# A retention layer and a bilinear feed-forward layer on one core: 36 uniform chunks instead of 40, stages placed back from their deadline, a rearranged opening, and q and k transposed by crossbar DMA from chunk 9 on

## The chip, the cores and the metric

The kernel runs on one core of one Trainium2 chip. The metric is device time in microseconds (us). A "run" is one execution; each kernel was executed several times on the same chip as the kernel before. The "span" of a profile is the time from the first to the last instruction in it; the time of the profiled run is about 2 us longer.

## The reference

There are 8 batches of 576 positions, with 8 heads of 64. First comes a retention layer (attention without softmax, with a decay per head), then a feed-forward layer in which two projections are multiplied:

```python
scores = (1 / sqrt(64)) * q @ k.transpose(0, 1, 3, 2)
gamma  = 1 - 2.0 ** (-5 - arange(8))                  # one per head
rel    = pos[:, None] - pos[None, :]
Dmat   = where(rel >= 0, gamma ** rel, 0)             # causal decay
x      = (scores * Dmat) @ v                          # -> [4608 tokens, 512]
out    = ((x @ w_a) * (x @ w_b)) @ w_out              # d_ff = 1536
```

Everything arrives and leaves as float32. The kernel computes in bfloat16.

## The kernel before

The kernel handles retention in chunks of positions. The decay is split into a factor per row of v (`vs`), a factor per column of the output (`qs`), and a 0/1 causal mask, so a chunk needs: a cast of q, k and v to bf16; q and k transposed (eight 128x128 transposes on PE into one PSUM tile, then a copy to SBUF); the running state `kv` (k times v, summed over earlier chunks of the batch); the scores; the mask multiply on DVE; the outputs (from scores, and from the state); and the multiply by `qs` that writes `xT`. 576 is 4.5 times 128, so each batch has four full chunks and a half one: 40 chunks.

The feed-forward layer takes tokens in blocks. `pa` and `pb` are the two projections, `po` the last one. It is called the dense part below. One unit is one matmul with 512 columns; a block of 512 tokens has 144 units, all of them 1296. The stages of later chunks are interleaved into the dense part: a list `todo` says after how many units which stage is put into PE's stream. In the first block the places are fixed by hand, in the later ones they are spread evenly.

```python
NCH = (S + 127) // 128
chunks = [(b, c, c * 128, min(128, S - c * 128))
          for b in range(B) for c in range(NCH)]

def transposes(i, act):
    ...                                   # cut: names
    tp = ps_att.tile([128, 2, HP, 128], BF16, tag="att", name="tp")
    for p in range(HP):
        for w, src in ((0, qb), (1, kb)):
            nc.tensor.transpose(tp[:, w, p, 0:n],
                                src[0:n, p * 128:(p + 1) * 128],
                                identity[0:n, 0:n])
    qkT = qkt_pool.tile([128, 2, HP, 128], BF16, tag="qkT", name="qkT")
    if act:
        nc.scalar.copy(qkT[:, :, :, 0:n], tp[:, :, :, 0:n])
    else:
        nc.vector.tensor_copy(qkT[:, :, :, 0:n], tp[:, :, :, 0:n])

# the opening: chunks 0 to 3, before the dense part
cast(0, early=True)                       # early: q on ACT, k on DVE
transposes(0, act=True)
for p in range(1, HP):
    make_qs(p)
state(0)
scores(0)
for i in range(1, 4):
    cast(i, early=True)
    ...                                   # cut: weight load
    transposes(i, act=True)
    flush()                               # the masks and xT multiplies put off
    outputs(i - 1)
    state(i)
    scores(i)
    flush()
...                                       # cut: weight loads
outputs(3)
flush()

# stages of the later chunks (after the first block), spread evenly over the block before theirs
gap = total / max(1, len(mine))
for m in range(len(mine)):
    p0 = m * gap
    todo += [(p0 + 0.03 * gap, "T", m), (p0 + 0.25 * gap, "S", m),
             (p0 + 0.85 * gap, "A", m)]   # transposes, scores, outputs
```

## Time and profile before

| | before |
|---|---|
| time, median (lowest to highest of 4 runs) | 390.06 us (388.33 to 390.63) |
| span of the profile | 386.2 us |
| first dense matmul | 26.9 us |
| PE transposes | 320 matmuls, 23.8 us busy |
| a 512-token block of the dense part, with the stages in it | 36.8 to 38.5 us with two groups of two chunks, 35.6 us in the last with only three chunks, 44.3 and 44.4 us where three groups of chunks fall in it |

These are lines of the page of the kernel before. In the first, the columns are busy time, share of the span and number of instructions for each engine. The next cut the span into 40 equal slices: busy share of PE in tenths, and the clock that the throttle granted to TensorE, in tenths. The last is the chain of work that ended last, by engine.

```profile
PE 351.9 (91%) x2736; PEld 188.3 (49%) x2736; DVE 169.9 (44%) x294; ACT 126.0 (33%) x242; POOL 91.4 (24%) x131
...
PE   2669996998979889899999998999998989999995
...
PEclk9999999899999999999999999999999999999999
...
PE 89%; DVE 7%; issue 1%; ACT 1%; DMA 1%; SPq 0%; DVEq 0%
```

PE is the bottleneck: what takes time away from PE, or waits away from before it, is worth its whole size. The waits of PE follow, from the view that lists who waited for whom: engine and line that waited, what it waited for, us in total, number of times, longest.

```profile
PE pa L275 <- DVE xT L262: 10.4, 8, 2.0
PE tp L188 <- ACT qb L170: 9.2, 4, 4.8
PE o L248 <- DVE sT L231: 6.3, 8, 2.0
```

The first line is the start of a block: its first `pa` matmul needs the last `xT`. The chain in order of time (start, us, what) shows one such start:

```profile
229.51 1.85 PE po L297 x8
...
231.38 0.69 DVE osb L308
232.07 0.61 DVE xT L262
...
232.72 1.02 PE pa L275 x4
```

The `xT` multiply was put off and stands behind the copy `osb` in DVE's queue. PE needs both to be done and stands still for 1.38 us.

### The profile page before, as it was taken

The numbers are of one execution on the slowest core, as the hardware profiler recorded it, in microseconds if no ns is written. First come the engines' busy times: TensorE is split into PE (matmuls) and PEld (weight loads), VectorE is DVE, ScalarE is ACT, GpSimd is POOL, SyncE is SP. The second block draws the span as 40 slices with busy tenths as digits, with TensorE's granted clock in tenths as the row PEclk, the third lists the DMA queues.
The fourth block names the chain that finished last, engine by engine and source line by source line (L and its number), as shares of the span: only waits on it lengthen the run. The fifth ranks groups of instructions, "written<-read, shape, count | busy, mean of one in ns | idle before, by whom it ended". The sixth has DMA issues, their size and how long they took to land.

```text
span 386.2 us, 6892 instructions
## 1 busy us (share of the span) xinstructions
PE 351.9 (91%) x2736; PEld 188.3 (49%) x2736; DVE 169.9 (44%) x294; ACT 126.0 (33%) x242; POOL 91.4 (24%) x131
## 2 busy tenths in 40 slices
PE   2669996998979889899999998999998989999995
PEld 1444454866744544445454544454544544444442
DVE  4443434344734454455335623662455444523321
ACT  6523322523414422234142414231433214312320
POOL 2640355413430430404132221122140300000000
PEclk9999999899999999999999999999999999999999
DMA  9999999957939902890268029602820020011002
GB/s 179 188 206 207 182 223 192 259 99 161 195 93 205 168 1 81 161 196 0 83 147 168 2 81 186 129 3 81 187 47 0 30 81 2 0 49 61 3 20 89
DMA packets 122512, 42.91 MB, mean 111 GB/s; under 512 B 113264, under 2 KB 117872, under 8 KB 122480
## 3 DMA queue, kind: packets, MB, share of 16 engines
q1 hardware_dynamic: 117728, 37.76, 46.5%
q0 software_dynamic: 4752, 4.72, 7.6%
q8 instruction: 21, 0.34, 0.4%
q14 instruction: 11, 0.09, 0.1%
HBM read 37.75 MB, written 9.44 MB: 122 GB/s over the span
## 4 chain that ended last, share of the span: by engine, by line
PE 89%; DVE 7%; issue 1%; ACT 1%; DMA 1%; SPq 0%; DVEq 0%
PE pa L275 25%; PE po L297 25%; PE pb L285 24%; PE tp L188 5%; PE o L248 3%; DVE xT L262 2%; PE kv L208 2%; PE o L256 2%; DVE sT L231 2%; DVE osb L308 1%; DMA kf<-in_k_dram 1%; DVE hT L290 1%; ACT qs L133 1%; DVE kb L171 0%; ACT qb L170 0%
## 5 line engine op out<-in xcount | busy, mean ns | idle before, releaser
L290 DVE TENSOR_TENSOR hT<-ha,pb 128x512 bf16<-128x512 bf16 (+1 forms) x120 | 76.1, 634 | 117.0 <-PE pb L285 115.0
L275 PE MATMUL pa<-xT,wa_sb 128*128 128x512 bf16 (+1 forms) x480 | 114.3, 361 | 10.5 <-DVE xT L262 10.4
L281 ACT CAST ha<-pa 128x512 bf16<-128x512 f32 (+1 forms) x120 | 65.0, 542 | 159.2 <-PE pa L275 159.0
L285 PE MATMUL pb<-xT,wb_sb 128*128 128x512 bf16 (+1 forms) x480 | 114.0, 360 | 0.2 <-ACT ha L281 0.2
L297 PE MATMUL po<-wo_sb,hT 128*128 128x512 bf16 x432 | 97.5, 380 | 0.0
L175 POOL TENSOR_TENSOR vb<-vf,vs 128x512 bf16<-128x512 f32 (+1 forms) x40 | 41.6, 1040 | 162.6 <-PE o L248 110.2
L275 PEld LDWEIGHTS <-wa_sb 128*128 128x128 bf16 x480 | 45.0, 98 | 53.9 <-issue 13.2
L285 PEld LDWEIGHTS <-wb_sb 128*128 128x128 bf16 x480 | 47.3, 98 | 47.8 <-issue 1.4
L297 PEld LDWEIGHTS <-hT 128*128 128x128 bf16 x432 | 40.5, 98 | 47.3
L308 DVE COPY osb<-po 128x512 f32<-128x512 f32 x18 | 12.5, 692 | 54.1 <-PE po L297 54.1
L262 DVE TENSOR_TENSOR xT<-o,qs 128x512 bf16<-128x512 f32 (+1 forms) x40 | 24.7, 631 | 23.1 <-PE o L256 18.0
L173 POOL CAST qb<-qf 128x512 bf16<-128x512 f32 (+1 forms) x36 | 21.9, 607 | 41.6 <-DMA qf<-in_q_dram 20.9
L188 PE MATMUL tp<-identity,qb 128*128 128x128 bf16 (+1 forms) x160 | 22.1, 228 | 9.2 <-ACT qb L170 9.2
L193 ACT COPY qkT<-tp 128x1024 bf16<-128x1024 bf16 (+1 forms) x23 | 21.2, 920 | 26.2 <-PE tp L188 26.2
L306 ACT COPY osb<-po 128x512 f32<-128x512 f32 x18 | 10.5, 585 | 57.4 <-PE po L297 57.4
L188 PE MATMUL tp<-identity,kb 128*128 128x128 bf16 (+1 forms) x160 | 21.8, 227 | 1.8 <-DVE kb L171 1.8
L174 POOL CAST kb<-kf 128x512 bf16<-128x512 f32 (+1 forms) x36 | 22.0, 611 | 6.3 <-DMA kf<-in_k_dram 3.7
L248 PE MATMUL o<-sT,vb 128*64 128x128 bf16 (+1 forms) x320 | 17.1, 226 | 6.3 <-DVE sT L231 6.3
L188 PEld LDWEIGHTS <-qb 128*128 128x128 bf16 (+1 forms) x160 | 15.4, 103 | 13.9 <-ACT qb L170 10.0
L248 PEld LDWEIGHTS <-vb 128*64 128x64 bf16 (+1 forms) x320 | 11.1, 114 | 15.2 <-issue 14.8
L188 PEld LDWEIGHTS <-kb 128*128 128x128 bf16 (+1 forms) x160 | 15.7, 104 | 3.9 <-DVE kb L171 2.4
L195 DVE COPY qkT<-tp 128x1024 bf16<-128x1024 bf16 (+1 forms) x17 | 10.9, 641 | 10.0 <-PE tp L188 9.4
(206 smaller groups left out, 181.7 us busy)
## 6 DMA issues: line engine op xcount, KB each, us to landing
out_dram<-osb SPq DMA_DIRECT2D x36, 256.0 KB, 2.0
qf<-in_q_dram SPq DMA_DIRECT2D x32, 256.0 KB, 4.9
kf<-in_k_dram SPq DMA_DIRECT2D x32, 256.0 KB, 5.0
vf<-in_v_dram SPq DMA_DIRECT2D x32, 256.0 KB, 5.1
wo_sb<-in_moe_w_out_dram POOLq DMA_DIRECT2D x3, 512.0 KB, 17.3
qf<-in_q_dram SPq DMA_DIRECT2D x8, 128.0 KB, 4.9
kf<-in_k_dram SPq DMA_DIRECT2D x8, 128.0 KB, 4.5
vf<-in_v_dram SPq DMA_DIRECT2D x8, 128.0 KB, 4.4
```

The lines of the kernel that those rows point to most:

```text
L173: nc.gpsimd.tensor_copy(qb[0:n, :], qf[0:n, :])
L174: nc.gpsimd.tensor_copy(kb[0:n, :], kf[0:n, :])
L175: nc.gpsimd.tensor_tensor(vb[0:n, :].rearrange("p (h d) -> p h d", h=H), vf[0:n, :].rearrange("p (h d) -> p h d", h=H), vs[0:n, c, :].unsq ...
L188: nc.tensor.transpose(tp[:, w, p, 0:n], src[0:n, p * 128:(p + 1) * 128], identity[0:n, 0:n])
L193: nc.scalar.copy(qkT[:, :, :, 0:n], tp[:, :, :, 0:n])
L248: nc.tensor.matmul(o[64 * hi:64 * hi + 64, p, 0:n], vb[0:n, e0:e0 + 64], sT[0:n, hi, p, 0:n], start=(p == 0), stop=(c == 0), skip_group_ch ...
L262: later.append(lambda: nc.vector.tensor_tensor(xT[:, :, t0:t0 + n], o[:, :, 0:n], qs[:, :, s0:s0 + n], op=ALU.mult))
L275: nc.tensor.matmul(pa[:, 0:n], wa_sb[:, c, fs], xT[:, c, tok0:tok0 + n], start=(c == 0), stop=(c == NC - 1))
L281: nc.scalar.copy(ha[:, 0:n], pa[:, 0:n])
L285: nc.tensor.matmul(pb[:, 0:n], wb_sb[:, c, fs], xT[:, c, tok0:tok0 + n], start=(c == 0), stop=(c == NC - 1))
L290: nc.vector.tensor_tensor(hT[:, F, 0:n], ha[:, 0:n], pb[:, 0:n], op=ALU.mult)
L297: nc.tensor.matmul(po, hT[:, F, u * 128:(u + 1) * 128], wo_sb[:, F, :], start=(F == 0), stop=(F == NF - 1))
```

## The change

It does four things. (1) Chunks of 128 run over two batches at a time, so 1152 positions make nine chunks, the middle one half from each batch, with a mask of its own. (2) The opening is one loop, and the copies out of PSUM are split, q on ACT and k on DVE. (3) Each stage from chunk 9 on is placed counting back from its block: outputs 16 units before the block starts, scores 36 units before that, casts 104 before. Chunks 4 to 8 get fixed positions. (4) From chunk 9 on, one DMA per chunk transposes q and k through the crossbar, from SBUF to SBUF.

```diff
-    NCH = (S + 127) // 128
+    NCH = NTOK // 128
+    PER = 2 * S // 128
+    MID = PER // 2
...                                        (cut: rows of a chunk, two-part loads)
+    def turn(i):
+        qkT = qkt_pool.tile([128, 2, HP, 128], BF16, tag="qkT", name="qkT")
+        nc.sync.dma_start_transpose(
+            qkT.rearrange("p w c s -> p (w c) s"),
+            natural[i][0].rearrange("p w d -> p (w d)"))
+        transposed[i] = qkT
...                                        (in transposes)
-        if act:
-            nc.scalar.copy(qkT[:, :, :, 0:n], tp[:, :, :, 0:n])
+        if how == "both":
+            nc.scalar.copy(qkT[:, 0], tp[:, 0])
+            nc.vector.tensor_copy(qkT[:, 1], tp[:, 1])
...                                        (opening; casts of chunk 0 before it)
+    for i in range(4):
+        transposes(i, "both")
+        scores(i)
+        state(i)
+        flush()
+        if i < 3:
+            cast(i + 1, early=True)
+        outputs(i)
+        flush()
...                                        (stages of the later chunks)
+    FIRST_TURNED = 9
+    def ahead(upto, early=False):
+        while counts["cast"] <= min(upto, NCH - 1):
+            i = counts["cast"]
+            cast(i, early)
+            counts["cast"] += 1
+            if counts["load"] < NCH:
+                load(counts["load"])
+                counts["load"] += 1
+            if i >= FIRST_TURNED:
+                turn(i)
...
+    for i in range(NCH - 1, 8, -2):
+        g = (i, i + 1) if i + 1 < NCH else (i,)
+        third = min(starts[i] - 16, limit - 60)
+        limit = third
+        second = third - (26 if i == 9 else 36)
+        todo += [(max(176, third - 104), ahead, (g[-1],)),
+                 (second - 16, first_stage, (g,)),
+                 (second, second_stage, (g,)),
+                 (third, third_stage, (g,))]
+    for i, first, second, third in (
+            (4, 117, 122, 129), (5, 134, 138, 143), (6, 147, 151, 158),
+            (7, 160, 164, 172), (8, 175, 179, 188)):
+        todo += [(first, one_by_one, ("T", i)), (second, one_by_one, ("S", i)),
+                 (third, one_by_one, ("A", i))]
```

In the first block, the `pa` matmuls of 3, 4 and 5 column groups run before the matching `pb`. Blocks are 512, 256, 384, 384, then 512, where before had 512, 256, 256, then 512.

More of the change, by code (lines that the diff above doesn't have):

```diff
@@ L47, with rows_of @@
     gammas = [1.0 - 2.0 ** (-5.0 - h) for h in range(H)]
-    NCH = (S + 127) // 128
-    chunks = [(b, c, c * 128, min(128, S - c * 128))
-              for b in range(B) for c in range(NCH)]
-    NTB = NTOK // 512
+    NCH = NTOK // 128
+    PER = 2 * S // 128
+    MID = PER // 2
+    HALF = S - 128 * MID
+    assert HALF == 64 and NTOK % (2 * S) == 0
+    def rows_of(i):
+        b, m = 2 * (i // PER), i % PER
+        if m < MID:
+            return [(0, 128, b, 128 * m)]
+        if m == MID:
+            return [(0, 64, b, 128 * m), (64, 64, b + 1, 0)]
+        return [(0, 128, b + 1, 64 + 128 * (m - MID - 1))]
     def pool(name, bufs, space=None):
@@ L61 @@
     nat = pool("nat", 5)
-    qkt_pool = pool("qkt", 4)
+    qkt_pool = pool("qkt", 6)
     st_pool = pool("st", 4)
     h_pool = pool("hT", 2)
-    ha_pool = pool("ha", 3)
+    ha_pool = pool("ha", 6)
     o_pool = pool("osb", 4)
@@ L85, in load @@
     def load(i):
-        if i >= len(chunks):
+        if i >= NCH:
             return
-        b, c, s0, n = chunks[i]
         tiles = []
@@ L91, in load @@
             t = stage.tile([128, DM], FP32, tag=name, name=name)
-            nc.sync.dma_start(
-                t[0:n, :].rearrange("p (h d) -> p h d", h=H),
-                src[b, :, s0:s0 + n, :].rearrange("h s d -> s h d"))
+            for r0, n, b, s0 in rows_of(i):
+                nc.sync.dma_start(
+                    t[r0:r0 + n, :].rearrange("p (h d) -> p h d", h=H),
+                    src[b, :, s0:s0 + n, :].rearrange("h s d -> s h d"))
             tiles.append(t)
@@ L99 @@
         load(i)
+    idxp_i = const.tile([128, PER], INT32)
+    nc.gpsimd.iota(idxp_i[:, 0:MID + 1], pattern=[[128, MID + 1]], base=0,
+                   channel_multiplier=1)
+    nc.gpsimd.iota(idxp_i[:, MID + 1:PER], pattern=[[128, PER - MID - 1]],
+                   base=64, channel_multiplier=1)
+    idx_i = const.tile([128, S + 64], INT32)
+    nc.gpsimd.iota(idx_i[:, 0:S], pattern=[[1, S]], base=0,
+                   channel_multiplier=0)
+    nc.gpsimd.iota(idx_i[:, S:S + 64], pattern=[[1, 64]], base=0,
+                   channel_multiplier=0)
     identity = const.tile([128, 128], BF16)
     make_identity(nc, identity)
-    idxp_i = const.tile([128, NCH], INT32)
-    nc.gpsimd.iota(idxp_i, pattern=[[128, NCH]], base=0, channel_multiplier=1)
-    idx_i = const.tile([128, S], INT32)
-    nc.gpsimd.iota(idx_i, pattern=[[1, S]], base=0, channel_multiplier=0)
     mask = const.tile([128, 128], BF16)
@@ L113 @@
         base=0, pattern=[[1, 128]], channel_multiplier=-1)
-    idxp_f = const.tile([128, NCH], FP32)
-    nc.vector.tensor_copy(idxp_f, idxp_i)
-    vs = const.tile([128, NCH, H], FP32)
-    for h in range(H):
-        nc.scalar.activation(vs[:, :, h], idxp_f, AF.Exp,
-                             bias=0.0, scale=-math.log(gammas[h]))
+    mask2 = const.tile([128, 128], BF16)
+    nc.gpsimd.tensor_copy(mask2, mask)
+    nc.gpsimd.memset(mask2[0:64, 64:128], 0.0)
     lgp = const.tile([128, HP], FP32)
@@ L127 @@
     nc.vector.memset(biasq, math.log(scale))
-    idx_f = const.tile([128, S], FP32)
+    idxp_f = const.tile([128, PER], FP32)
+    nc.vector.tensor_copy(idxp_f, idxp_i)
+    nc.vector.tensor_scalar_add(idxp_f[64:128, MID:MID + 1],
+                                idxp_f[64:128, MID:MID + 1], -float(S))
+    vs = const.tile([128, PER, H], FP32)
+    for h in range(H):
+        nc.scalar.activation(vs[:, :, h], idxp_f, AF.Exp,
+                             bias=0.0, scale=-math.log(gammas[h]))
+    idx_f = const.tile([128, S + 64], FP32)
     nc.vector.tensor_copy(idx_f, idx_i)
-    qs = const.tile([128, HP, S], FP32)
+    qs = const.tile([128, HP, S + 64], FP32)
     def make_qs(c):
@@ L134, in make_qs @@
                              bias=biasq[:, 0:1], scale=lgp[:, c:c + 1])
-    make_qs(0)
     states = [const.tile([128, HP, 128], BF16, name=f"state{i}")
@@ L162, in cast @@
     def cast(i, early=False):
-        if i >= len(chunks):
-            return
-        b, c, s0, n = chunks[i]
         qf, kf, vf = staged.pop(i)
-        qb, kb, vb = (nat.tile([128, DM], BF16, tag=t, name=t)
-                      for t in ("qb", "kb", "vb"))
+        qkb = nat.tile([128, 2, DM], BF16, tag="qkb", name="qkb")
+        vb = nat.tile([128, DM], BF16, tag="vb", name="vb")
+        qb, kb = qkb[:, 0], qkb[:, 1]
         if early:
-            nc.scalar.copy(qb[0:n, :], qf[0:n, :])
-            nc.vector.tensor_copy(kb[0:n, :], kf[0:n, :])
-        else:
-            nc.gpsimd.tensor_copy(qb[0:n, :], qf[0:n, :])
-            nc.gpsimd.tensor_copy(kb[0:n, :], kf[0:n, :])
+            nc.scalar.copy(qb, qf)
+            nc.vector.tensor_copy(kb, kf)
+        else:
+            nc.gpsimd.tensor_copy(qb, qf)
+            nc.gpsimd.tensor_copy(kb, kf)
@@ L175, in cast @@
         nc.gpsimd.tensor_tensor(
-            vb[0:n, :].rearrange("p (h d) -> p h d", h=H),
-            vf[0:n, :].rearrange("p (h d) -> p h d", h=H),
-            vs[0:n, c, :].unsqueeze(2).to_broadcast([n, H, D]),
+            vb.rearrange("p (h d) -> p h d", h=H),
+            vf.rearrange("p (h d) -> p h d", h=H),
+            vs[:, i % PER, :].unsqueeze(2).to_broadcast([128, H, D]),
             op=ALU.mult)
-        natural[i] = (qb, kb, vb)
-    def transposes(i, act):
-        b, c, s0, n = chunks[i]
-        qb, kb, vb = natural[i]
-        tp = ps_att.tile([128, 2, HP, 128], BF16, tag="att", name="tp")
-        for p in range(HP):
-            for w, src in ((0, qb), (1, kb)):
-                nc.tensor.transpose(tp[:, w, p, 0:n],
-                                    src[0:n, p * 128:(p + 1) * 128],
-                                    identity[0:n, 0:n])
-        qkT = qkt_pool.tile([128, 2, HP, 128], BF16, tag="qkT", name="qkT")
-        if act:
-            nc.scalar.copy(qkT[:, :, :, 0:n], tp[:, :, :, 0:n])
+        natural[i] = (qkb, qb, kb, vb)
@@ new lines, in turn, with transposes @@
+    def turn(i):
[4 more added lines that the diff above has]
+        transposed[i] = qkT
+    def transposes(i, how):
+        qkb, qb, kb, vb = natural[i]
+        tp = ps_att.tile([128, 2, HP, 128], BF16, tag="att", name="tp")
+        for w, src in ((0, qb), (1, kb)):
+            for p in range(HP):
+                nc.tensor.transpose(tp[:, w, p, :],
+                                    src[:, p * 128:(p + 1) * 128], identity)
+        qkT = qkt_pool.tile([128, 2, HP, 128], BF16, tag="qkT", name="qkT")
+        if how == "both":
+            nc.scalar.copy(qkT[:, 0], tp[:, 0])
+            nc.vector.tensor_copy(qkT[:, 1], tp[:, 1])
+        elif how == "act":
+            nc.scalar.copy(qkT, tp)
@@ L194, in transposes @@
         else:
-            nc.vector.tensor_copy(qkT[:, :, :, 0:n], tp[:, :, :, 0:n])
+            nc.vector.tensor_copy(qkT, tp)
         transposed[i] = qkT
     def state(i):
-        b, c, s0, n = chunks[i]
-        if c == NCH - 1:
+        m = i % PER
+        if m == PER - 1:
             return
-        qb, kb, vb = natural[i]
-        if c == 0:
-            kv_of[b] = ps_kv.tile([128, HP, 128], FP32, tag="kv", name="kv")
-        kv = kv_of[b]
+        qkb, qb, kb, vb = natural[i]
+        r = slice(64, 128) if m == MID else slice(0, 128)
@@ L206, in state @@
+        if m == 0 or m == MID:
+            kv_of[0] = ps_kv.tile([128, HP, 128], FP32, tag="kv", name="kv")
+        kv = kv_of[0]
         for p in range(HP):
             sl = slice(p * 128, (p + 1) * 128)
-            nc.tensor.matmul(kv[:, p, :], kb[0:n, sl], vb[0:n, sl],
-                             start=(c == 0 and p == 0), stop=True,
+            nc.tensor.matmul(kv[:, p, :], kb[r, sl], vb[r, sl],
+                             start=(m in (0, MID) and p == 0), stop=True,
                              skip_group_check=True)
@@ L216, in scores @@
     def scores(i):
-        b, c, s0, n = chunks[i]
         qkT = transposed[i]
@@ L225, in scores @@
                 r = slice(64 * hi, 64 * hi + 64)
-                nc.tensor.matmul(ps[hi][0:n, p, 0:n], qkT[r, 1, p, 0:n],
-                                 qkT[r, 0, p, 0:n], start=True, stop=True,
+                nc.tensor.matmul(ps[hi][:, p, :], qkT[r, 1, p, :],
+                                 qkT[r, 0, p, :], start=True, stop=True,
                                  skip_group_check=True)
+        keep = mask2 if i % PER == MID else mask
         def masked(hi):
             nc.vector.tensor_tensor(
-                sT[0:n, hi, :, 0:n], ps[hi][0:n, :, 0:n],
-                mask[0:n, 0:n].unsqueeze(1).to_broadcast([n, HP, n]),
+                sT[:, hi], ps[hi],
+                keep.unsqueeze(1).to_broadcast([128, HP, 128]),
                 op=ALU.mult)
@@ L239, in outputs @@
     def outputs(i):
-        b, c, s0, n = chunks[i]
-        qb, kb, vb = natural.pop(i)
+        m = i % PER
+        qkb, qb, kb, vb = natural.pop(i)
         qkT = transposed.pop(i)
@@ L247, in outputs @@
                 e0 = p * 128 + 64 * hi
-                nc.tensor.matmul(o[64 * hi:64 * hi + 64, p, 0:n],
-                                 vb[0:n, e0:e0 + 64], sT[0:n, hi, p, 0:n],
-                                 start=(p == 0), stop=(c == 0),
+                nc.tensor.matmul(o[64 * hi:64 * hi + 64, p, :],
+                                 vb[:, e0:e0 + 64], sT[:, hi, p, :],
+                                 start=(p == 0), stop=(m == 0),
                                  skip_group_check=True)
-        if c > 0:
+        if m > 0:
             st = state_of.pop(i)
+            n = 64 if m == MID else 128
             for p in range(HP):
@@ L260, in outputs @@
                                      skip_group_check=True)
-        t0 = b * S + s0
+        s0 = rows_of(i)[0][3]
         later.append(lambda: nc.vector.tensor_tensor(
-            xT[:, :, t0:t0 + n], o[:, :, 0:n], qs[:, :, s0:s0 + n],
+            xT[:, :, i * 128:(i + 1) * 128], o, qs[:, :, s0:s0 + 128],
             op=ALU.mult))
-    blocks = [512, 256, 256] + [512] * ((NTOK - 1024) // 512)
-    def ffn_block(tok0, n):
+    blocks = [512, 256, 384, 384] + [512] * ((NTOK - 1536) // 512)
@@ L270, in ffn_block @@
+    WCOLS = [3, 4, 5]
+    def ffn_block(tok0, n, runs):
         hT = h_pool.tile([128, NF, 512], BF16, tag="h", name="hT")
-        for F in range(NF):
-            fs = slice(F * 128, (F + 1) * 128)
-            pa = ps_ffn.tile([128, 512], FP32, tag="ab", name="pa")
-            for c in range(NC):
-                nc.tensor.matmul(pa[:, 0:n], wa_sb[:, c, fs],
-                                 xT[:, c, tok0:tok0 + n],
-                                 start=(c == 0), stop=(c == NC - 1))
-                if c < NC - 1:
-                    yield n / 512, False
-            ha = ha_pool.tile([128, 512], BF16, tag="ha", name="ha")
-            nc.scalar.copy(ha[:, 0:n], pa[:, 0:n])
-            yield n / 512, False
-            pb = ps_ffn.tile([128, 512], FP32, tag="ab", name="pb")
-            for c in range(NC):
-                nc.tensor.matmul(pb[:, 0:n], wb_sb[:, c, fs],
-                                 xT[:, c, tok0:tok0 + n],
-                                 start=(c == 0), stop=(c == NC - 1))
-                if c < NC - 1:
-                    yield n / 512, False
-            nc.vector.tensor_tensor(hT[:, F, 0:n], ha[:, 0:n], pb[:, 0:n],
-                                    op=ALU.mult)
-            pop()
-            yield n / 512, True
@@ new lines, in ffn_block @@
+        f0 = 0
+        for count in runs:
+            has = {}
+            for F in range(f0, f0 + count):
+                fs = slice(F * 128, (F + 1) * 128)
+                pa = ps_ffn.tile([128, 512], FP32, tag="ab", name="pa")
+                for c in range(NC):
+                    nc.tensor.matmul(pa[:, 0:n], wa_sb[:, c, fs],
+                                     xT[:, c, tok0:tok0 + n],
+                                     start=(c == 0), stop=(c == NC - 1))
+                    if c < NC - 1:
+                        yield n / 512, False
+                ha = ha_pool.tile([128, 512], BF16, tag="ha", name="ha")
+                nc.scalar.copy(ha[:, 0:n], pa[:, 0:n])
+                has[F] = ha
+                yield n / 512, False
+            for F in range(f0, f0 + count):
+                fs = slice(F * 128, (F + 1) * 128)
+                pb = ps_ffn.tile([128, 512], FP32, tag="ab", name="pb")
+                for c in range(NC):
+                    nc.tensor.matmul(pb[:, 0:n], wb_sb[:, c, fs],
+                                     xT[:, c, tok0:tok0 + n],
+                                     start=(c == 0), stop=(c == NC - 1))
+                    if c < NC - 1:
+                        yield n / 512, False
+                nc.vector.tensor_tensor(hT[:, F, 0:n], has[F][:, 0:n],
+                                        pb[:, 0:n], op=ALU.mult)
+                pop()
+                yield n / 512, True
+            f0 += count
@@ L315 @@
     gate = const.tile([1, 64], BF16)
+    make_qs(0)
+    make_qs(1)
     cast(0, early=True)
-    transposes(0, act=True)
-    for p in range(1, HP):
-        make_qs(p)
-    state(0)
-    scores(0)
-    for i in range(1, 4):
-        cast(i, early=True)
-        if i == 2:
-            load_w(0, 384)
-        transposes(i, act=True)
-        flush()
-        outputs(i - 1)
-        state(i)
-        scores(i)
+    make_qs(2)
+    for i in range(4):
+        transposes(i, "both")
+        if i == 0:
+            make_qs(3)
+        scores(i)
+        state(i)
+        flush()
+        if i < 3:
+            if i == 2:
+                load_w(0, 128 * WCOLS[0])
+            cast(i + 1, early=True)
+        outputs(i)
         flush()
-    load_w(384, 896)
-    load_w(896, DFF)
+    load_w(128 * WCOLS[0], 128 * (WCOLS[0] + WCOLS[1]))
+    load_w(128 * (WCOLS[0] + WCOLS[1]), DFF)
     for i in (0, 1, 2):
         load_wo(i)
-    outputs(3)
-    flush()
     nc.sync.dma_start(gate, wo_sb[0:1, 7, 0:64])
@@ L340, with total @@
         load(i)
-    groups = [[4, 5], [6], [7, 8], [9, 10], [11, 12]]
-    groups += [[i for i in (j, j + 1) if i < len(chunks)]
-               for j in range(13, len(chunks), 2)]
-    first_token = [b * S + s0 for b, c, s0, n in chunks]
-    counts = {"cast": 4, "load": 8}
-    def run(what, g):
-        if what == "T":
-            while counts["cast"] <= min(g[-1] + 2, len(chunks) - 1):
-                cast(counts["cast"])
-                counts["cast"] += 1
-                if counts["load"] < len(chunks):
-                    load(counts["load"])
-                    counts["load"] += 1
-            transposes(g[0], act=True)
-            if len(g) > 1:
-                transposes(g[1], act=False)
-            state(g[0])
+    def total(n):
+        return NF * 2 * NC * n / 512 + NF * n / 128
@@ new lines @@
+    starts, at = {}, 0.0
+    tok = 0
+    for n in blocks:
+        for i in range(tok // 128, (tok + n) // 128):
+            starts[i] = at
+        tok += n
+        at += total(n)
+    counts = {"cast": 4, "load": 8}
+    FIRST_TURNED = 9
[9 more added lines that the diff above has]
+                turn(i)
@@ L361, in run, with first_stage, second_stage, third_stage @@
+    def first_stage(g):
+        state(g[0])
+    def second_stage(g):
+        for i in g[1:]:
+            state(i)
+        for i in g:
+            scores(i)
+    def third_stage(g):
+        flush()
+        for i in g:
+            outputs(i)
+    def one_by_one(what, i):
+        if what == "T":
+            ahead(i, early=True)
+            transposes(i, "both")
         elif what == "S":
-            if len(g) > 1:
-                state(g[1])
-            for i in g:
-                scores(i)
+            scores(i)
+            state(i)
@@ L366, in run @@
         else:
             flush()
-            for i in g:
-                outputs(i)
-    tok0 = 0
-    for tb, n in enumerate(blocks):
-        mine = []
-        if tb + 1 < len(blocks):
-            end = tok0 + n + blocks[tb + 1]
-            while groups and first_token[groups[0][0]] < end:
-                mine.append(groups.pop(0))
-        total = NF * 2 * NC * n / 512 + NF * n / 128
-        if tb == 0:
-            todo = [(108, "T", 0), (122, "S", 0), (138, "T", 1),
-                    (140, "A", 0), (143, "S", 1), (144, "A", 1)]
-        else:
-            gap = total / max(1, len(mine))
-            todo = []
-            for m in range(len(mine)):
-                p0 = m * gap
-                todo += [(p0 + 0.03 * gap, "T", m), (p0 + 0.25 * gap, "S", m),
-                         (p0 + 0.85 * gap, "A", m)]
-        at = 0.0
-        for cost, edge in ffn_block(tok0, n):
+            outputs(i)
@@ new lines @@
+    todo = []
+    limit = 1e9
+    for i in range(NCH - 1, 8, -2):
[12 more added lines that the diff above has]
+                 (third, one_by_one, ("A", i))]
@@ L391 @@
+    todo.sort(key=lambda e: e[0])
+    at = 0.0
+    tok = 0
+    for tb, n in enumerate(blocks):
+        runs = WCOLS if tb == 0 else [1] * NF
+        for cost, edge in ffn_block(tok, n, runs):
             at += cost
             while todo and edge and at >= todo[0][0]:
-                _, what, m = todo.pop(0)
-                run(what, mine[m])
-        for _, what, m in todo:
-            run(what, mine[m])
+                _, fn, args = todo.pop(0)
+                fn(*args)
         flush()
-        tok0 += n
+        tok += n
```

## The prediction

> **What bounds it now.** TensorE: PE is busy 91% of the 386.2 us span and holds 89% of the chain of waits. By the timeline: (1) Opening, 0 to 26.9 us: chunks 0 to 3 pass transpose, copy, scores, mask, outputs one after the other; PE waits 13 us there, and its 128-column matmuls are spaced 106 ns against 55 ns later. (2) Dense matmuls (pa, pb, po): 1296 units of 512 columns at 216 ns, 280 us. (3) Attention of the other 36 chunks in between: transposes 0.45 us per chunk, kv 0.22, scores 0.23, outputs 0.24 and 0.23; with slow-clock stretches and waits about 60 us. (4) Tail, 3.8 us. The waits list: first dense matmul of a block on the last xT multiply, 10.4 us in 8; output matmuls on the mask multiply, 6.3 us in 8.
>
> **What the change does.**
> - 36 chunks in place of 40. A half chunk costs PE nearly a full one (it reloads as many weights). 4 x 1.37 = about -5 us.
> - PE transposes gone for 27 chunks: 27 x 0.45 = -12 us, on the critical path. The PSUM copies that go with them (0.64 us DVE, 0.92 us ACT) were mostly off it.
> - Stages placed back from the deadline, the third 16 units (3.5 us) before the block: nearly all xT waits and most mask waits go, with the slow clock after them (transposes at 106 ns spacing at 68.6 us): about -12 us.
> - Opening: cadence of chunks 4.1 us instead of 4.9, copies split over ACT and DVE, but two qs activations ahead of the first cast, and load issues of 1.15 us each: dense part starts near 24 us, -3 us.
> - Added: 27 crossbar DMAs of 256 KB. The Trainium skill ("DMA: Bandwidth & Descriptors", Latency and other measured facts) states 261 GB/s for DMA transposes: an estimate of 1.0 us of data each, plus the 2.0 us that a 256 KB store needs to land: 3 to 5 us, with loads ahead on the queue 6 to 10. No run shows it yet. The lead is 68 units, 14.7 us, before scores need it; casts take 4.5 us per pair on POOL. It fits, with some spill: +3 us.
>
> **Sum.** 24 opening + 280 dense + 5 restarts after interruptions (0.97 against 0.86 us per four) + 30 attention (32 x 0.93) + 2 for five chunks transposed on PE + 4 remaining waits + 4 tail = 349 us span; measured times are 4 us over the span (390.2 against 386.2): **353 us**, range 345 to 367. Faster by over 2%: 0.94; within 2%: 0.04; slower: 0.02.
>
> **What would show each step.** 72 transposes of about 10 us in place of 320 of 44 us; first pa matmul at 23 to 25 us; waits of pa on xT under 2 us; mask waits under 3 us; a steady 512-token block of 35 us instead of 37 to 38; transposing DMAs landing in under 10 us, and no large wait of score matmuls on qkT. POOL unchanged, about 90 us.
>
> **What would make it wrong.** Transposing DMAs that take over 8 us each, or hold the SP queue: it issues loads and stores in order, so a late transpose delays the next loads, and PE waits on qkT at each of 13 pairs. Loads that fall behind between 60 and 100 us, where the DMA share is already 0.8 to 1.0. Weights not landed when the dense part starts earlier. An opening that is slower because the qs activations precede the first cast.

## More of the kernel before

The transposes are two groups of instructions (busy us, mean ns of one):

```profile
L188 PE MATMUL tp<-identity,qb 128*128 128x128 bf16 (+1 forms) x160 | 22.1, 228 | 9.2 <-ACT qb L170 9.2
L188 PE MATMUL tp<-identity,kb 128*128 128x128 bf16 (+1 forms) x160 | 21.8, 227 | 1.8 <-DVE kb L171 1.8
```

The two groups alternate on PE and overlap, so their busy times must not be added: together they cover 23.8 us, not the 43.9 us of the sum (the prediction and e1's expectation used the sum). Even 23.8 us overstates them, since they overlap other matmuls too: in the chain, the 16 transposes of a pair of chunks hold PE for 0.89 us.

## The result, and the profile after

| | before | after |
|---|---|---|
| time, median (lowest to highest of 4 runs each) | 390.06 us (388.33 to 390.63) | 366.63 us (366.24 to 367.12) |
| span of the profile | 386.2 us | 364.5 us |
| first dense matmul | 26.9 us | 26.3 us |
| PE waits after that | 16.5 us | 9.7 us |
| of these up to 4 us into the third block | 4.5 us | 9.7 us |
| later | 12.0 us | none |
| a steady 512-token block | 36.8 to 38.5 us | 35.1 to 35.6 us |

Waits are gaps of over 0.15 us in front of a matmul. The trace after has 2390 matmuls for 2424 weight loads, so 34 matmul records are missing; eight gaps of 0.16 to 0.22 us that the view of waits puts down to "issue" are such holes and are not counted.

The ratio is 0.9407 (95% interval 0.9375 to 0.9439). Ratios here are the mean time of one kernel's fast runs over that of the other's of the same rounds, so not quite the ratio of the medians that are quoted. The kernel before had medians from 388.1 to 390.1 us in the four sets of runs, so kernels from different sets are compared by their ratios; a step of 0.01 is 3.9 us.

The page after, the same lines:

```profile
PE 335.3 (92%) x2390; PEld 174.8 (48%) x2424; DVE 164.0 (45%) x279; ACT 115.1 (32%) x234; POOL 77.5 (21%) x113
...
PE   2669998686999999999999999999999999999995
...
PEclk9999999699999999999999999999999999999999
...
PE 88%; DVE 7%; ACT 3%; issue 2%; DVEq 0%
```

From the eleventh slice on (91 us) PE is at 9 in every slice, where before had eights to the end. All that is missing is in the first ten slices, and the clock has a dip in the eighth, deeper than the one of before in the same slice. The waits of PE:

```profile
PE o L276 <- DVE sT L259: 7.3, 16, 1.4
PE tp L213 <- ACT qkb L188: 5.8, 2, 5.3
PE tp L213 <- DVE qkb L189: 2.1, 3, 0.9
PE pa L309 <- DVE xT L291: 1.6, 2, 0.8
```

No line says that PE waited for a crossbar DMA. The wait of `pa` on `xT` is nearly gone; that of the outputs on the mask has not shrunk. The start of a steady block in the chain has no DVE in it any more:

```profile
221.81 2.81 PE po L335 x13
224.62 0.86 PE pa L309 x4
```

The transposes left on PE, and the crossbar DMAs as the DMA view lists them (count, then median us from issue to landing):

```profile
L213 PE MATMUL tp<-identity,qkb 128*128 128x128 bf16 x72 | 8.2, 270 | 8.1 <-ACT qkb L188 5.8 <-DVE qkb L189 2.1
```

```profile
qkT<-qkb SPq DMA_TRANSPOSE x27, 4.5
```

The crossbar did its part. The gain is smaller than predicted, mostly because of what happens before 103 us. In the opening, the chain shows one link that the prediction did not have. This is chunk 1:

```profile
10.16 1.03 PE tp L213 x8
11.22 0.59 ACT qkT L217
11.83 0.44 DVE qkT L218
12.32 0.39 PE sc_241 L253 x2
...
12.97 1.29 DVE sT L259 x2
```

The two copies of `qkT`, split over two engines, run one after the other, 0.59 and then 0.44 us: as long as the one ACT copy of before (1.01 us). The next transposes start at 15.3 us, 5.1 us after these.

The second place is 62 to 67 us, at the end of the first block. PE in order of time (start, us, engine, line, what; in brackets how long it stood still before, and for whom):

```profile
62.72 1.03 PE L335 MATMUL po<-wo_sb,hT 128*128 128x512 bf16 x4
65.13 0.24 PE L276 MATMUL o<-sT,vb 128*64 128x128 bf16 x1 [1.38 <-DVE sT L259]
65.72 0.38 PE L276 MATMUL o<-sT,vb 128*64 128x128 bf16 x7 [0.35 <-DVE sT L259]
...
67.11 0.91 PE L309 MATMUL pa<-xT,wa_sb 128*128 128x256 bf16 x4 [0.78 <-DVE xT L291]
```

From 63.75 to 67.1 us PE does less than 1 us of work. The view of stretches (stretch, its length, then busy us and instructions of PE, PEld, DVE, ACT and POOL, granted clock, DMA share, GB/s) says what came after:

```profile
54.00:67.00 13.00, 9.01 (x96) 4.73 (x95) 6.61 (x12) 3.74 (x8) 3.49 (x4) 1.00 1.11 247
67.00:80.00 13.00, 10.90 (x99) 7.57 (x99) 5.66 (x13) 4.75 (x12) 6.43 (x9) 0.74 0.89 191
```

For 13 us the granted clock averaged 0.74. The whole dip lies in 6.8 us at half the clock:

```profile
67.30:74.10 6.80, 6.07 (x40) 3.86 (x39) 2.02 (x4) 2.29 (x6) 3.04 (x5) 0.50 0.98 217
```

In the kernel before the clock was at half for 3.4 us, from 67.1 us. The DMA engines are full of loads in the first of these stretches (share 1.11), so there are two readings of the waits at 54 to 93 us: the stages of chunks 4 to 8 stand too close together for the in-order queues of ACT and DVE, or the loads come too late. The experiments tell them apart.

### The profile page after: what moved, and what is told of

Its sections match the earlier page's. It is cut to its first block, busy times and chain, and to the rows that moved or that the text cites. A ratio compares the mean times of both kernels' runs of the same rounds, so it can differ in the third digit from the quotient of the medians.

```text
span 364.5 us, 6162 instructions
## 1 busy us (share of the span) xinstructions
PE 335.3 (92%) x2390; PEld 174.8 (48%) x2424; DVE 164.0 (45%) x279; ACT 115.1 (32%) x234; POOL 77.5 (21%) x113
## 3 DMA queue, kind: packets, MB, share of 16 engines
q1 hardware_dynamic: 146240, 44.84, 62.8%
## 4 chain that ended last, share of the span: by engine, by line
PE 88%; DVE 7%; ACT 3%; issue 2%; DVEq 0%
PE pa L309 25%; PE po L335 25%; PE pb L322 24%; PE o L276 3%; DVE sT L259 3%; PE o L285 2%; PE kv L236 2%; PE tp L213 2%; ACT qkT L217 1%; DVE hT L327 1%; DVE qkT L218 1%; DVE osb L346 1%; DVE xT L291 1%; ACT qs L154 0%; DVE qkb L189 0%
## 5 line engine op out<-in xcount | busy, mean ns | idle before, releaser
L327 DVE TENSOR_TENSOR hT<-ha,pb 128x512 bf16<-128x512 bf16 (+2 forms) x120 | 76.0, 634 | 110.7 <-PE pb L322 100.7
L309 PE MATMUL pa<-xT,wa_sb 128*128 128x512 bf16 (+2 forms) x472 | 113.3, 364 | 2.4 <-DVE xT L291 1.6
L322 PE MATMUL pb<-xT,wb_sb 128*128 128x512 bf16 (+2 forms) x471 | 111.6, 360 | 0.7 <-DVE hT L327 0.3
L315 ACT CAST ha<-pa 128x512 bf16<-128x512 f32 (+2 forms) x120 | 65.1, 542 | 131.9 <-PE pa L309 119.4
L193 POOL TENSOR_TENSOR vb<-vf,vs 128x512 bf16<-128x512 f32 x36 | 37.5, 1042 | 178.4 <-issue 83.0
L291 DVE TENSOR_TENSOR xT<-o,qs 128x512 bf16<-128x512 f32 x36 | 24.2, 685 | 9.6 <-PE o L285 8.4
L276 PE MATMUL o<-sT,vb 128*64 128x128 bf16 x288 | 16.7, 231 | 7.4 <-DVE sT L259 7.3
L191 POOL CAST qkb<-qf 128x512 bf16<-128x512 f32 x27 | 16.5, 610 | 21.2 <-PE kv L236 16.3
L276 PEld LDWEIGHTS <-vb 128*64 128x64 bf16 x288 | 11.0, 114 | 16.3 <-issue 13.1
L192 POOL CAST qkb<-kf 128x512 bf16<-128x512 f32 x27 | 16.6, 614 | 2.0 <-DMA kf<-in_k_dram 2.0
L236 PE MATMUL kv<-vb,qkb 128*128 128x128 bf16 (+1 forms) x128 | 13.5, 233 | 0.1
```

The source lines that it names most:

```text
L191: nc.gpsimd.tensor_copy(qb, qf)
L192: nc.gpsimd.tensor_copy(kb, kf)
L193: nc.gpsimd.tensor_tensor(vb.rearrange("p (h d) -> p h d", h=H), vf.rearrange("p (h d) -> p h d", h=H), vs[:, i % PER, :].unsqueeze(2).to_ ...
L236: nc.tensor.matmul(kv[:, p, :], kb[r, sl], vb[r, sl], start=(m in (0, MID) and p == 0), stop=True, skip_group_check=True)
L276: nc.tensor.matmul(o[64 * hi:64 * hi + 64, p, :], vb[:, e0:e0 + 64], sT[:, hi, p, :], start=(p == 0), stop=(m == 0), skip_group_check=True)
L291: later.append(lambda: nc.vector.tensor_tensor(xT[:, :, i * 128:(i + 1) * 128], o, qs[:, :, s0:s0 + 128], op=ALU.mult))
```

## The experiments

Twelve kernels were run, each correct against the reference.

### What the crossbar is worth: e1 and e3

e1 is the changed kernel with every transpose on PE; e3 is the kernel before with the crossbar from chunk 11 on (29 chunks) and only what that needs: q and k cast into one tile, and six buffers for `qkT` instead of four.

```diff
 e1, in the changed kernel
-    FIRST_TURNED = 9
+    FIRST_TURNED = 99
     def first_stage(g):
+        transposes(g[0], "act")
+        if len(g) > 1:
+            transposes(g[1], "dve")
         state(g[0])

 e3, in the kernel before
+    FIRST_TURNED = 11
+    def turn(i): ...                 # one crossbar DMA, as in the change
     def transposes(i, act):
+        if i >= FIRST_TURNED:
+            return
 (and turn(i) after the cast and load of each chunk from 11 on)
```

> The changed kernel with its 36 chunks, its opening and its stage positions, but all transposes on PE (a pair's in its first stage, copied out by ACT and DVE). Theory: the crossbar's whole gain is the PE time that it takes away, 27 x 0.45 us = 12 us, so 379 us here (377 to 381), with transposes of 36 x 8 = 288 matmuls about 42 us busy. Rival A: the crossbar DMAs delay loads and cause part of the waits at 54 to 93 us, then less than 8 us comes back (under 375 us). Rival B: the copies out of PSUM bring waits of their own, then over 15 us (above 382 us).

> The kernel before (40 chunks, its opening and its stage positions), with chunks 11 to 39 transposed by crossbar DMA instead of on PE, and nothing else. Theory: the crossbar's gain is PE time and needs nothing of the rest of the change: 29 chunks of 0.40 to 0.45 us = 12 to 13 us, so 376 to 378 us, ratio about 0.968. Rival: it pays only with stages placed back from the deadline; then less than 6 us here, or waits of scores on qkT.

e1 took 379.26 us, ratio 0.9757 (0.9732 to 0.9782), with 288 transposes of 22.5 us busy, not the 42 expected; PE waits 9.7 us after the opening, as in the change, so the crossbar DMAs are not what it waits for. e3 took 376.16 us, ratio 0.968 (0.964 to 0.972), with PE's waits as before (10.4 us on `xT`, 6.3 us on the masks). Put on the kernel before, the crossbar is worth 0.032, or 12.4 us. Taken from the changed kernel it costs 0.035, or 13.6 us. 27 x 0.45 us is 12.2 us, and 13.1 us for the 29 chunks of e3: the gain is PE's time, and it depends on nothing else in the change. The other three parts together are worth 0.024, or 9.5 us. The prediction had counted about 20 us for them.

### Is the crossbar near its limit: e7

```diff
         nc.sync.dma_start_transpose(qkT..., natural[i][0]...)
+        spare = spare_pool.tile([128, 2, HP, 128], BF16, tag="spare", name="spare")
+        nc.sync.dma_start_transpose(spare..., natural[i][0]...)   # nobody reads it
```

> The changed kernel, with each crossbar DMA issued twice, the second into a spare tile that nobody reads. Theory: from 103 us on the crossbar has room to spare on the SP queue and on the DMA engines, so doubling it costs nothing there; only at chunks 9 to 12, where the DMA engines are full of loads, scores wait for it: 367 to 371 us, no wait of scores on qkT after 130 us. Rival: the lead is just enough, then every pair waits and the time is above 376 us.

366.72 us, ratio 0.9418 (0.9397 to 0.944): the same as the changed kernel, and no wait of PE for a crossbar DMA even at chunks 9 to 12, where I had expected one. The share of the 16 DMA engines of the queue went from 62.8% to 73.4%:

```profile
q1 hardware_dynamic: 174752, 51.92, 73.4%
...
qkT<-qkb SPq DMA_TRANSPOSE x27, 4.5
spare<-qkb SPq DMA_TRANSPOSE x27, 3.3
```

So the 3 us of "spill" in the prediction were not there.

### The two copies: e2

```diff
         tp = ps_att.tile([128, 2, HP, 128], BF16, tag="att", name="tp")
+        tps = [tp, tp]
+        if how == "both":
+            tps[1] = ps_att.tile([128, 2, HP, 128], BF16, tag="att", name="tpk")
...                                   (q's transposes into tps[0], k's into tps[1])
             nc.scalar.copy(qkT[:, 0], tp[:, 0])
-            nc.vector.tensor_copy(qkT[:, 1], tp[:, 1])
+            nc.vector.tensor_copy(qkT[:, 1], tps[1][:, 1])
```

> The changed kernel, with q's and k's transposes of chunks 0 to 8 in two PSUM tiles instead of one, so that the DVE copy need not wait for the ACT copy. Theory: those two copies run one after the other (0.59 + 0.43 us) because they share a tile; apart they overlap, each of 9 chunks is 0.4 us shorter, the spacing of chunks in the opening falls from 5.1 to about 4.6 us and the first pa starts at 24.5 us instead of 26.3; total 363 to 365 us against 366.6. Rival: the opening is paced by the loads (1.15 us per issue, three per chunk), then first pa stays at 26 us and the time within 0.5 us.

361.21 us, ratio 0.9295 (0.9271 to 0.9319), 4.4 us better than the change. The copies overlap, from the timeline of e2:

```profile
10.23 0.59 ACT L221 COPY qkT<-tp 128x512 bf16<-128x512 bf16 x1 [0.70 <-PE tp L217]
10.66 0.42 DVE L222 COPY qkT<-tpk 128x512 bf16<-128x512 bf16 x1 [0.36 <-PE tpk L217]
```

The DVE copy now waits for PE and not for ACT. The spacing of chunks is 4.5 us instead of 5.1, and the first dense matmul starts at 23.9 us. The span of the profile falls by 6.3 us: 2.4 in the opening, 0.6 in the first block, and 3.3 in the second, 28.5 us instead of 31.9, where the clock stayed full in this profile (and in four of the five runs). Those 3.3 us come from the clock (6.8 us at half of it cost 3.4 us) and not from shorter copies; PE's standstill at the end of the first block is still there (see e12). The destination is still one tile in SBUF, so it was the shared source that put the copies in order. The Trainium skill ("PSUM — Partial Sum Buffer", PSUM bank collisions raise a hardware error) says that any two engines that touch the same bank and quadrant at once collide, two readers included, and that schedulers therefore add a dependency between ACT and DVE there. The trace agrees as far as the order goes (11.9 us of waiting of the DVE copy for the ACT copy, 9 times); no run here raised the error.

### Chunks 4 to 8: e4

```diff
+        if what == "C":
+            ahead(i, early=True)              # casts, a step of their own
         elif what == "T":
-            ahead(i, early=True)
             transposes(i, "both")
-            (4, 117, 122, 129), (5, 134, 138, 143), (6, 147, 151, 158),
-            (7, 160, 164, 172), (8, 175, 179, 188)):
+            (4, 99, 106, 112, 125), (5, 116, 122, 128, 141),
+            (6, 137, 147, 155, 171), (7, 153, 163, 171, 187),
+            (8, 169, 179, 187, 203)):         # casts, transposes, scores, outputs
```

> The changed kernel, with chunks 4 to 8 cast 6 to 10 units before their transposes and their stages set 6 to 16 units apart instead of 4 to 9; crossbar, opening and loads untouched. Theory: the 8.8 us of PE waits from 54 to 103 us and the dip of the clock in there come from stages placed closer than the in-order queues of ACT and DVE can serve; waits there fall under 3 us, the clock stays full, time 358 to 361 us. Rival: the chunks' loads come too late (DMA share 1.0 there), then casts wait for loads instead, the waits stay near 9 us and the time within 2 us of 366.6.

360.18 us, ratio 0.9267 (0.9237 to 0.9298), 5.4 us better than the change. The placement was the cause of most of the waits: those of outputs on masks in the dense part fall from 4.9 to 1.5 us (the view's 3.8 includes 2.4 in the opening). But a new wait of one piece appears, which neither the theory nor the rival named:

```profile
PE o L276 <- DVE sT L259: 3.8, 10, 1.2
PE sc L253 <- DMA qkT<-qkb: 3.7, 1, 3.7
```

e4 casts these chunks earlier and also sets their stages further apart; which of the two does more is not separated. With PE ahead of time, scores of the pair 9 and 10 come before a crossbar DMA has landed. After it the clock dips again, in most of this kernel's runs: the fastest had a mean granted clock of 1.0 and took 358.1 us, the slowest 0.988 and 362.1 us.

### Does the standstill cause the slow clock: e12

```diff
     def outputs(i):
         o = ps_att.tile([128, HP, 128], FP32, tag="att", name="o")
+        if i == 5:                             # work for nothing, overwritten below
+            for _ in range(6):
+                nc.tensor.matmul(o.rearrange("p a b -> p (a b)"),
+                                 wa_sb[:, 0, 0:128], wb_sb[:, 0, 0:512],
+                                 start=True, stop=True, skip_group_check=True)
```

> The changed kernel, with six 512-column matmuls (1.3 us of work for nothing, written to a bank that the next matmuls overwrite) ahead of chunk 5's outputs, where PE stands still for 1.4 us at 64 us. Theory: the granted clock falls to 0.74 in the stretch from 67 to 80 us because PE stood nearly idle from 63.7 to 67.1 us; with that gap filled the clock stays full, the block that starts there takes 28.5 us instead of 31.9 and the time falls to 363 us, with more work on PE. Rival: the clock falls for another reason (the run of small matmuls, the DMA load), then the block stays at 31.9 us and the time at 366.6 us or a little more.

364.21 us, ratio 0.9382 (0.9364 to 0.94). The granted clock in the stretch after the filled gap was full:

```profile
67.00:80.00 13.00, 9.44 (x119) 7.05 (x118) 6.43 (x14) 5.07 (x13) 6.27 (x9) 1.00 0.89 198
```

The block that starts there took 29.7 us instead of 31.9, though not the 28.5 expected, and the first block grew by 1.7 us. In all four runs the mean clock was 0.998 or 0.999, against 0.990 to 0.995 in the four runs of the change. That is shown: keep PE busy there and the clock does not fall, at the same DMA share of 0.89. The time gained in all, 1.0 us by the ratios, is not clear of the noise, since the intervals of this kernel and of the change overlap. The dip is in line with the Trainium skill ("TensorE: Matmul & The Clock Gate", Part 1: The HAM clock gate), which says that the clock falls to half after an idle window of about 3.4 us and that the window is free-running: here PE was nearly idle for 3.4 us, and the same kernel dips in some runs and not in others (the six runs of e5 have mean clocks from 0.986 to 0.999).

A standstill alone is not enough. e2 and e5 have the same 3.4 us with 0.9 us of work in them (from 60.7 and 64.0 us), and no dip in their profiles. The dips last 3.41 us or 6.83 us in these traces. Count steps of 3.41 us from where the clock record of each trace becomes full (29.7 us in the change, 27.5 in e2, 31.0 in e5). In the change the standstill fills one step, from 63.8 to 67.3 us, with PE busy for 29% of it. In e2 and e5 it lies across two steps, and in the emptier one PE is busy for 52% and 55%. This fits the free-running window; no run shifted the standstill on purpose to test it.

### The opening: e5 and e5b

```diff
 e5, in the changed kernel
+    transposes(0, "both")
     for i in range(4):
-        transposes(i, "both")
         scores(i)
         state(i)
         flush()                               # masks
         cast(i + 1, early=True)
+        transposes(i + 1, "both")
         outputs(i)
         flush()

 e5b, against e5
         scores(i)
+        cast(i + 1, early=True)
         state(i)
         flush()
-        cast(i + 1, early=True)
         transposes(i + 1, "both")
         outputs(i)
-        flush()
+    flush()                                   # once, after the loop
```

> The changed kernel, with the next chunk's cast and transposes put ahead of a chunk's outputs on PE in the opening. Theory: the opening is one chain per chunk (transposes 1.03, copies 1.02, scores, masks 1.29, outputs 1.0); taking the outputs out of it brings the spacing from 5.1 to about 4.1 us, first pa at 23 us instead of 26.3, total 363 to 364 us. Rival: loads pace it, first pa after 25.5 us and time within 0.7 us.

> The changed kernel, with the next chunk's transposes ahead of a chunk's outputs on PE, as in the earlier trial, and in addition the next chunk's casts ahead of the masks on DVE and ahead of the state copies on ACT. Theory: the earlier trial gained only 0.7 us in the opening because the transposes then waited for the casts, which stood behind the masks; with the casts first the spacing of chunks falls from 4.8 to about 3.8 us, near the pace of the loads (3.5 us), and the first pa starts at 22.5 to 23.5 us instead of 25.7. Rival: the loads pace it already, then the first pa stays after 25 us.

e5 took 364.12 us, ratio 0.938 (0.9353 to 0.9408), not clear of the change's interval. The theory fell in the form in which I had it: the spacing is 4.8 us and the first dense matmul starts at 25.7 us, only 0.7 us earlier. PE's wait for the casts grew instead, from 5.8 to 10.8 us on the ACT cast, because the casts stood behind the masks and the state copies:

```profile
PE tp L213 <- ACT qkb L188: 10.8, 6, 5.3
```

e5b takes that away: the transposes of chunks 0 to 3 start at 5.3, 8.6, 12.2 and 16.8 us, and the first dense matmul at 22.7 us; 362.49 us, ratio 0.9315 (0.9288 to 0.9343). The casts now wait for k's DMA (5.4 us in the opening, against 1.4 us in the change), so the loads do pace it, as the rival said, but at 3.3 to 4.6 us and not at 5.1:

```profile
DVE qkb L189 <- DMA kf<-in_k_dram: 5.4, 4, 1.5
```

### The slack before a block: e6

```diff
-        third = min(starts[i] - 16, limit - 60)
+        third = min(starts[i] - 2, limit - 60)
```

> The changed kernel, with the third stage of chunks 9 to 35 placed 2 units ahead of its block instead of 16 (all stages of those chunks move with it). Theory: the 16 units of slack are what took the wait of pa on xT away; it comes back at some 1.4 us (before had 1.38) in each of the 7 blocks from the fourth on, with a little clock loss: 374 to 378 us. Rival: the order within the block matters and not the slack: waits of pa on xT stay under 3 us in all and the time under 369 us.

369.72 us, ratio 0.95 (0.948 to 0.952), 3.6 us worse than the change. It lies between the two expectations. The waits of `pa` on `xT` come back, as 4.5 us in 8 waits of at most 0.8 us, not 1.4 us each: the outputs of both chunks are then put into PE's stream after the last `po`, so PE works while DVE is at `osb`.

```profile
PE pa L309 <- DVE xT L291: 4.5, 8, 0.8
```

The slack is worth 3.6 us, about a third of the 9.8 us (7 times 1.4) that I had credited it with.

### Together: e8, e10 and e11

e8 is e2 and e4 together, with each crossbar DMA issued before the load that stands next to it. e10 issues the loads of a pair after both of its crossbar DMAs. e11 adds e5b.

```diff
 e10, against e8
     def ahead(upto, early=False):
+        fetched = 0
...
             if i >= FIRST_TURNED:
                 turn(i)
-            if counts["load"] < NCH:
-                load(counts["load"]); counts["load"] += 1
+            fetched += 1
+        for _ in range(fetched):
+            if counts["load"] < NCH:
+                load(counts["load"]); counts["load"] += 1
```

> The two edits that helped, together (q and k transposed in two PSUM tiles; chunks 4 to 8 cast earlier with their stages further apart), and in the queue of SP each chunk's crossbar DMA ahead of the load issued at the same point. Theory: the two gains are separate (opening and waits at 54 to 93 us) and the 3.7 us wait for the crossbar of chunks 9 and 10 goes with the new order: 353 to 356 us, first pa at 24 us, PE waits after it under 4 us. Rival: the loads of chunks 9 to 12 are late whatever the order (DMA share 1.0 to 1.3 there), then PE waits 3 us or more before 105 us and the time is 357 us or more.

> The last combined kernel, with the loads of a pair issued after both of its crossbar DMAs. Theory: the 3.0 us wait of scores for the crossbar of chunk 10 is the order of SP's queue (its q and k were cast at 79.7 us, its crossbar was issued at 83.3 behind six loads), so the wait falls under 0.5 us and the time to 353 us. Rival: the DMA engines are full there (share 1.1), then the crossbar lands as late as before or the loads put off bring a wait later; 355.5 us or more.

> All that helped together: two PSUM tiles, chunks 4 to 8 apart, loads after both crossbar DMAs of a pair, and the opening with casts ahead of masks. If the opening trial holds: first pa at 22 to 23 us and 351 to 352 us. If the weights or chunks 4 to 7 then come too late (they are loaded after the weights, at a fixed time), the gain of the opening is lost in a wait before 60 us: 353 us or more.

e8: 356.12 us, ratio 0.9165 (0.9136 to 0.9194), with one wait of 3.0 us left for the crossbar of chunk 10:

```profile
PE sc L257 <- DMA qkT<-qkb: 3.0, 1, 3.0
```

e10: 354.38 us, ratio 0.9128 (0.9099 to 0.9156), and that wait is gone: it was the order of SP's queue, six loads ahead of the DMA that was needed, and not the DMA engines. In the timeline of SP's queue the second crossbar DMA of that pair starts at 83.31 us in e8 (first line), and in e10 both are issued in one piece from 76.83 us (second line):

```profile
83.31 1.28 SPq L203 DMA_TRANSPOSE qkT<-qkb  x1
76.83 3.41 SPq L203 DMA_TRANSPOSE qkT<-qkb  x2
```

The intervals of e8 and e10 overlap; the wait is what tells them apart. e11: 352.15 us (351.92 to 352.16), ratio 0.9062 (0.905 to 0.9073), first dense matmul at 23.5 us, clock 1.000. It beats the change by 0.0345, some 13 us. The edit of e5b brings the first dense matmul only 0.7 us forward here (24.1 to 23.5 us), against 3.7 us by itself, so it does not add up with the two tiles. In e11 the transposes of k wait 1.2 us in all for an `xT` multiply, which fits four PSUM buffers being short for five tiles; that was not tested and stays open. Lines of its page, to be read against those above:

```profile
PE 333.9 (95%) x2424; PEld 173.6 (50%) x2424; DVE 163.3 (47%) x279; ACT 115.5 (33%) x234; POOL 78.6 (22%) x113
...
PE   3779998999999999999999999999999999999995
...
PEclk9999999999999999999999999999999999999999
```

## Why the prediction was right or wrong

The time, 366.63 us, lies in the range (345 to 367) but at its very end, 13.6 us above the 353 us named. That it lies inside is luck in part: the profiled span is 15.5 us over the sum, the wide range covers most of that, and a last term that was itself 1.9 us too large covers the rest. The terms of the sum, with what the two profiles show (PE's time from each start to the next, waits taken out; rounded):

| term | before | predicted | after |
|---|---|---|---|
| opening, to the first dense matmul | 26.9 us | 24 us | 26.3 us |
| dense part with restarts | 286.5 us | 285 us | 287.7 us |
| attention work in it | 52.4 us | 32 us | 37.2 us |
| waits of PE in it | 16.5 us | 4 us | 9.7 us |
| tail | 3.9 us | 4 us | 3.7 us |
| span | 386.2 us | 349 us | 364.5 us |
| median time over the span of the profile | 3.9 us | 4 us | 2.1 us |

The last line of the prediction's sum was a comparison of different runs: the profiled run of before took 387.92 us, 1.7 us over its own span, and was faster than the others.

- **Bottleneck: right.** PE is 92% busy after, and the PE time that the crossbar removes came back in full (e1 and e3).
- **Crossbar, -12 us: right.** 12.4 us on the kernel before (e3), 13.6 us in the changed kernel (e1). Landing took 4.5 us in the median and 6.6 at most, under the 10 predicted. The spill of +3 us was wrong: doubling the DMAs cost nothing that the runs show (e7).
- **Four chunks fewer, -5 us: not tested by itself.** A kernel with the old schedule and the new chunks was not built. The nearest is e1, with all transposes on PE in the new schedule: its attention work in the dense part is 48.6 us for 32 chunks, against 52.4 us for 36 before.
- **Stages from the deadline, -12 us for the waits and the slow clock after them: the step that failed.** It holds for chunks 9 to 35: waits later than 4 us into the third block fell from 12.0 us to none, and a steady block takes 35.1 to 35.6 us as predicted (35). I had read the deadline rule as if it covered all chunks. Chunks 4 to 8 have fixed positions 4 to 9 units apart, 0.9 to 1.9 us, in which a cast, transposes, two copies that take turns, scores and two masks must pass through the in-order queues of ACT and DVE. Waits up to the third block rose from 4.5 to 9.7 us, and a standstill of 3.4 us brought 6.8 us at half the clock, twice as long as before (e4 and e12). In all, the waits fell by 6.8 us, from 16.5 to 9.7, and the time lost to the slow clock grew. "Mask waits under 3 us" was wrong: 7.3 us, 2.4 of them in the opening.
- **Opening, -3 us at a spacing of 4.1 us: the size was off.** It gave 0.6 us at a spacing of 5.1 us. "Copies split over ACT and DVE" was taken to mean at the same time; they shared a PSUM tile and ran in turn (e2: 0.6 us per chunk, 2.4 us at the first dense matmul).
- **Attention work, 32 us: 5.2 us too small.** Little of it is the stretch at the lower clock: in e2, where the clock stayed full, the attention work is still 36.0 us.
- **POOL unchanged at about 90 us: wrong,** 77.5 us. Four chunks fewer are 9 us of casts and v multiplies (0.61 + 0.61 + 1.04 us each), and the change moves the q and k casts of chunks 4 to 8, 6 us, to ACT and DVE; I had overlooked both.
- **Small miss in an experiment.** In e1 I expected 42 us busy for 288 transposes and got 22.5. The 43.9 us of before, from which that came, counts overlapping time twice (23.8 us without); in e1 the transposes of q and k are one group and are counted once. The "44 us" of the prediction is the same slip. The time of the kernel did come out as expected, since the 0.45 us per chunk was read from the chain.

That e11 lands at 352 us, near the figure predicted for the change, does not make the prediction better: it needed four edits that the change does not have (two PSUM tiles, chunks 4 to 8 apart, loads after both crossbar DMAs, casts ahead of masks).

## What to carry to other kernels

When work is split over two engines to shorten a chain, look in the trace whether the second one waits for the first: two readers of one PSUM tile took turns here, and a second tile brought the first dense matmul 2.4 us forward. When a schedule is given by a rule, ask which items the rule leaves out; nearly all that PE waited here after the opening, it waited in the stretch with five chunks placed by hand. In a queue that issues in order, put the DMA that somebody is about to wait for ahead of the prefetches, and do not count a standstill of PE only once: here one of 3.4 us was followed by 6.8 us at half the clock.

## What the Trainium skill lacked or had wrong

- "DMA: Bandwidth & Descriptors", Latency and other measured facts, states 261 GB/s for DMA transposes with a non-contiguous middle dimension, and 350 to 400 GB/s for contiguous ones. (The prediction took the first without its condition.) The 27 crossbar DMAs here (0.26 MB each, SBUF to SBUF) took 1.4 us of all 16 engines each (e7: the queue's share of the span grew from 62.8% of 364.5 us to 73.4% of 365.0 us for 27 more), or 1.75 us (against e1: 48.3% of 376.1 us). That is 150 to 180 GB/s while other traffic runs.
- "DMA: Bandwidth & Descriptors" gives the sequencer's time for a DMA transpose only for other sizes. Here one of 128 x 1024 elements held SP's queue for 1.2 to 4.1 us, 2.2 us in the median, and landed 3.0 to 6.6 us after issue.
- "TensorE: Matmul & The Clock Gate", Part 4: PE-mode transpose, gives about 275 ns for a 128x128 bf16 transpose in a kernel. The duration agrees (227 to 270 ns mean), but what a transpose costs a busy PE is its spacing, 55 ns at full clock (16 in 0.89 us) and 106 ns at the lower clock; the page does not say so there. It adds that the full clock does not engage for transposes; among dense matmuls they ran at it, as the 55 ns show.
- "PSUM — Partial Sum Buffer" warns that two readers of one bank collide, but not what keeping them apart costs: here 0.6 us per chunk of lost overlap.
